# Two more loads of K at the head of the load queue of a decode kernel

## The chip, the core and the metric

The kernel runs on one core of a Trainium2 chip. The metric is the device time in microseconds (us) of one execution.

## The reference, cut to what matters

One decode step for two sequences: layernorm, attention of one new token over the last 2048 positions of a K and V cache (32 heads of 192), an output projection with a residual, then a second layernorm and a gated feed-forward part with its residual.

```
B, Sq, D = 2, 1, 640;  Hq = Hkv = 32;  Sk, Dh = 8192, 192;  F = 1536;  W = 2048
def attention(x, k_cache, v_cache, wq, wo):
    q = (x @ wq).reshape(B, Sq, 32, 192).transpose(0, 2, 1, 3)
    k, v = k_cache[:, :, Sk - W:], v_cache[:, :, Sk - W:]
    p = softmax(einsum("bhqd,bhkd->bhqk", q, k) * 192 ** -0.5)
    return einsum("bhqk,bhkd->bhqd", p, v).transpose(0, 2, 1, 3).reshape(B, Sq, 6144) @ wo
h = x + attention(layernorm(x), ...)
out = h + (gelu(n @ w_gate) * (n @ w_up)) @ w_down        # n = layernorm(h)
```

All inputs and the output are bf16. K and V of the window are 2 x 32 x 2048 x 192 values each, 50.3 MB apiece.

## The kernel before, in words

**Groups.** The 64 pairs of sequence and head are worked off in 16 groups g of four heads. The window's 2048 positions of one head are cut into 32 runs of 64 positions (`TPG`), and one run, 64 x 192 values, is 24,576 contiguous bytes in memory. A group's K is thus 32 x 4 runs, and each of the 128 partitions of SBUF gets one run: `kv_src` (L369 to L371) builds the source as `"h (i t) d -> i h (t d)"`, the run number i outermost, the head h next, so partition 4i + h holds run i of head h. V is loaded in the same way.

**The ring.** All big loads go into one tile, `ring`: 147,456 bytes per partition, six slots of 24,576 (`SLOT`). `K_AT` (L234) puts the K of groups 0 to 3, modulo four, at slots 0, 1, 3 and 5; `V_AT` puts V at slots 2 and 4. Wq (61,440 bytes per partition, `load_wq`) lies from the middle of slot 3 to the end of slot 5. Wo and the feed-forward weights later take slots that K and V have left.

**What sets the order.** The program is recorded first (`P.op`) and then emitted engine by engine; waits are worked out from what each operation reads and writes. `load` (L347) puts a load into a list. `pump` takes loads from its head, in order, as long as the ring space that they need is not held by a load that is still to be used; `done` marks a load as used and calls `pump` again. Every load in the ring is issued by SP (recorded at L363), on one queue, in the list's order. SP waits before an issue until what it overwrites is free: for the readers of the old contents, and, where a load lands on space that another load has written and nobody reads, for that other load's completion. The wait stands on SP, so all later issues stand behind it.

**The order of loads.** K(0), Wq, K(1), V(0), then K(g+1) and V(g) in turn, a quarter of Wo after every fourth group, and the feed-forward weights at the end. K(2) lands on space of Wq, so SP issues it only when PE has used Wq.

**Beside SP.** ACT's queue issues two small loads: the first fifth of W_gate (L394) and x (L431). POOL and DVE build constants (identities, masks) in the first 17 us. PE transposes each K group as pairs of bf16 (L574), DVE (L588) and ACT (L584) copy it out of PSUM; q is projected once from Wq (L598, in `q_rows`); scores, softmax and the product with V follow group by group; `oproj` adds a quarter of the output projection, then comes the feed-forward part. One store of the output (L878) ends the kernel: `out[:, 0, :].rearrange("b (r n) -> r b n", r=4)`, four blocks of two rows, from 8 partitions.

The list of loads begins (L430 to L434):

```
        load_wg0()
        P.op("act", lambda e: e.dma_start(xrow[0:2, :], A_x[:, 0, :]), W=["xrow"], dma="dx")
        load_k(0)
        load_wq()
        load_k(1)
```

## Time and profile before

| | |
|---|---|
| median of 2 runs | 292.64 us (292.55 to 292.73) |
| the profiled execution's own time | 292.58 us |
| its span, first to last instruction | 291.3 us |
| busy share of PE, PE weight loads, DVE, ACT, POOL | 68%, 51%, 42%, 26%, 9% |
| DMA packets | 6506, 122.44 MB, 420 GB/s over the span |
| read from memory | 122.29 MB |
| K loads, V loads | 16 and 16 of 3072 KB each |

Times below are in us from the start of the span. The page cuts the span into 40 slices of 7.3 us; each digit is a busy share in tenths, and a row GB/s gives what the 16 DMA engines moved. The DMA queue of SP is q1, that of ACT q10. SPq is SP's issuing of a DMA; the time behind it is that of the issue, not of the transfer. A DMA is split into packets: here one packet for each contiguous run of a load, and a small one for each DMA engine that reports its part as complete. In the timeline, what stands in brackets is how long the engine was idle before the row, and what ended that.

### The profile page before, as it was taken

The numbers are of one execution on the slowest core, as the hardware profiler recorded it, in microseconds if no ns is written. First come the engines' busy times: TensorE is split into PE (matmuls) and PEld (weight loads), VectorE is DVE, ScalarE is ACT, GpSimd is POOL, SyncE is SP. The second block draws the span as 40 slices with busy tenths as digits, with TensorE's granted clock in tenths as the row PEclk, the third lists the DMA queues.
The fourth block names the chain that finished last, engine by engine and source line by source line (L and its number), as shares of the span: only waits on it lengthen the run. The fifth ranks groups of instructions, "written<-read, shape, count | busy, mean of one in ns | idle before, by whom it ended". The sixth has DMA issues, their size and how long they took to land.

```text
span 291.3 us, 5093 instructions
## 1 busy us (share of the span) xinstructions
PE 198.6 (68%) x2141; PEld 147.6 (51%) x2141; DVE 122.8 (42%) x231; ACT 76.9 (26%) x72; POOL 25.7 (9%) x85
## 2 busy tenths in 40 slices
PE   0650868786668288768677478868478778496684
PEld 0640437566355175637374475645465746472341
DVE  4350025455435334635356244635247445253331
ACT  1050014333322122423222123523142333151001
POOL 8820073000000000000000000000000000000000
PEclk9997568999979869997989579999689799688957
DMA  8999999999999999999999999999999999999994
GB/s 324 432 440 422 428 432 432 428 429 429 428 419 440 432 432 432 429 432 432 432 416 448 432 432 430 432 412 429 432 432 425 422 432 432 429 432 434 420 411 181
DMA packets 6506, 122.44 MB, mean 420 GB/s; under 512 B 734, under 2 KB 864, under 8 KB 1504
## 3 DMA queue, kind: packets, MB, share of 16 engines
q1 hardware_dynamic: 6348, 121.90, 97.8%
q10 hardware_dynamic: 148, 0.40, 0.4%
q8 instruction: 7, 0.11, 0.2%
q14 instruction: 3, 0.02, 0.0%
HBM read 122.29 MB, written 0.00 MB: 420 GB/s over the span
## 4 chain that ended last, share of the span: by engine, by line
DMA 73%; PE 18%; DVE 3%; issue 2%; SPq 2%; ACT 1%; DVEq 0%
DMA ring<-in_A_k_cache_dram 54%; PE tpp L574 13%; DMA ring<-in_A_wq_dram 10%; DMA ring<-in_B_w_down_dram 9%; DVE ktr L588 3%; PE tpp L598 2%; SPq L363 2%; PE ops L680 1%; DVE ering L428 1%; ACT ktr L584 1%; PE m L731 1%; PE m L713 1%; PE m L871 0%; PE m L694 0%; DVE yrow L877 0%
## 5 line engine op out<-in xcount | busy, mean ns | idle before, releaser
L574 PE MATMUL tpp<-identf,ring 128*128 128x128 f32 x768 | 116.2, 314 | 39.3 <-DMA ring<-in_A_k_cache_dram 25.2
L574 PEld LDWEIGHTS tpp<-identf,ring 128*128 128x128 f32 x768 | 102.8, 163 | 47.5 <-DMA ring<-in_A_k_cache_dram 26.5
L588 DVE COPY ktr<-tpp 128x2048 bf16<-128x2048 bf16 x64 | 78.4, 1224 | 91.4 <-PE tpp L574 91.4
L584 ACT ACTIVATE ktr<-tpp 128x2048 bf16<-128x2048 bf16 x32 | 60.1, 1877 | 94.9 <-PE tpp L574 94.9
L655 ACT ACTIVATE eexp<-sm,nm 128x512 bf16<-128x512 f32 x16 | 11.6, 722 | 71.7 <-DVE nm L653 71.7
L635 PE MATMUL sps<-ktr,rq 128*16 128x512 bf16 x384 | 25.7, 402 | 1.1 <-POOL rq L428 1.1
L680 PE MATMUL ops<-ring,ering 128*32 128x384 bf16 x512 | 25.0, 339 | 0.0
L644 DVE CUSTOM_DVE_ANT_1 sm<-sps,mska 128x512 f32<-128x512 f32 x16 | 11.0, 686 | 27.0 <-issue 27.0
L428 POOL TENSOR_TENSOR rq<-qs,mask 128x96 bf16<-128x96 bf16 x16 | 5.5, 354 | 175.6 <-PE sps L635 154.1
L680 PEld LDWEIGHTS ops<-ring,ering 128*32 128x32 bf16 x512 | 12.7, 99 | 8.5 <-issue 2.8
L635 PEld LDWEIGHTS sps<-ktr,rq 128*16 128x16 bf16 x384 | 8.9, 89 | 14.4 <-issue 5.5
L651 PEld LDWEIGHTS m<-mrhs,pm 128*128 128x128 bf16 x16 | 1.5, 96 | 22.9 <-DVE mrhs L424 22.9
L651 PE MATMUL m<-mrhs,pm 128*128 128x16 bf16 x16 | 2.9, 184 | 14.8 <-DVE mrhs L424 14.8
L598 PE MATMUL tpp<-ring,xnT 128*32 128x384 bf16 x80 | 6.1, 499 | 9.4 <-DMA ring<-in_A_wq_dram 9.4
L598 PEld LDWEIGHTS tpp<-ring,xnT 128*32 128x32 bf16 x80 | 3.4, 143 | 11.9 <-issue 9.6
L621 DVE CAST qs<-ops 128x384 bf16<-128x384 f32 x1 | 0.6, 558 | 15.8 <-PE ops L616 15.8
L428 DVE TENSOR_TENSOR ering<-m,mask 128x256 bf16<-128x256 f32 x16 | 6.6, 415 | 1.3 <-PE m L664 1.3
L713 PE MATMUL m<-selb,orow 128*128 128x2 bf16 x48 | 3.5, 200 | 5.2 <-DVE ering L428 4.5
L713 PEld LDWEIGHTS m<-selb,orow 128*128 128x128 bf16 x48 | 3.2, 159 | 6.0 <-DVE ering L428 4.9
L664 PE MATMUL m<-sel,eexp 128*128 128x64 bf16 x64 | 4.8, 200 | 1.2 <-ACT eexp L655 1.2
L494 PE MATMUL m<-identb,xrow 2*128 2x2 bf16 x5 | 0.3, 173 | 7.4 <-DMA xrow<-in_A_x_dram 7.4
L428 DVE TENSOR_TENSOR orow<-m,wm 128x1536 bf16<-128x1536 f32 x3 | 5.3, 1751 | 0.0
(127 smaller groups left out, 93.6 us busy)
## 6 DMA issues: line engine op xcount, KB each, us to landing
ring<-in_A_k_cache_dram SPq DMA_DIRECT2D x16, 3072.0 KB, 29.5
ring<-in_A_v_cache_dram SPq DMA_DIRECT2D x16, 3072.0 KB, 25.4
ring<-in_A_wq_dram SPq DMA_DIRECT2D x1, 7680.0 KB, 28.1
ring<-in_A_wo_dram SPq DMA_DIRECT2D x4, 1920.0 KB, 21.6
ring<-in_B_w_gate_dram SPq DMA_DIRECT2D x1, 1536.0 KB, 31.4
ring<-in_B_w_up_dram SPq DMA_DIRECT2D x1, 1536.0 KB, 21.9
ring<-in_B_w_down_dram SPq DMA_DIRECT2D x1, 960.0 KB, 24.3
ring<-in_B_w_down_dram SPq DMA_DIRECT2D x1, 480.0 KB, 25.0
```

The lines of the kernel that those rows point to most:

```text
L363: P.op("sp", lambda e, v=v, src=src: e.dma_start(v, src), W=toks + [("sem", sem)], dma=sem)
L428: return lambda e: e.tensor_tensor(out=out, in0=a, in1=b, op=op)
L574: ins = e.transpose(tpp[bi][:, 512 * j + 128 * u:512 * j + 128 * (u + 1)], kv[:, off:off + 128], identf[:, :])
L584: act(lambda e, dst=dst, bv=bv: e.activation(out=dst, in_=bv, func=ACT.Copy), W=[("kt", half, k)], X=both)
L588: dve(lambda e, dst=dst, bv=bv: e.tensor_copy(dst, bv.rearrange("p (a x) -> p a x", a=2)), W=[("kt", half, k)], X=both, cls=0)
L598: ins = e.matmul(tps[0][32 * r:32 * (r + 1), 0:384], lhsT=xnT[:, c, 32 * J:32 * (J + 1)], rhs=wq[:, c, 1536 * J + 384 * r:1536 * J + 384 * ...
L635: ins = e.matmul(sps[32 * ch:32 * ch + 16, :], lhsT=rq[:, g % 4, k, :], rhs=ktr[:, k // 2, 1024 * ch + k % 2:1024 * (ch + 1):2], start=(k ...
L644: dve(lambda e: e.tensor_tensor_reduce(out=sm[:, :].rearrange("p (u x) -> p u x", u=4), in0=sps[:, :].rearrange("p (u x) -> p u x", u=4), ...
L655: act(lambda e: e.activation(out=eexp[:, :], in_=sm[:, :], func=ACT.Exp, bias=nm[:, 0:1], scale=1.0, accum_out=zr[:, g % 4:g % 4 + 1]), R= ...
L664: ins = e.matmul(o, lhsT=eexp[:, 128 * u:128 * (u + 1)], rhs=sel64[:, :], start=True, stop=True)
L680: ins = e.matmul(ops_[32 * r:32 * (r + 1), 0:384], lhsT=ering[:, g % 4, t, :], rhs=vv[:, 384 * t:384 * (t + 1)], start=(g % 4 == 0 and t < 4),
L713: ins = e.matmul(m2[:, 2 * kk:2 * kk + 2], lhsT=orow[:, :, kk:DH:12], rhs=selb[:, :], start=True, stop=True)
```

## The change

Two loads are put at the head of the list, ahead of `load_wg0()`:

```
+        runs = A_k_cache[0, 0:8, SKT - WIN:, :].rearrange("h (i t) d -> h i (t d)", t=2 * TPG)
+        load("p0", 0, 2 * SLOT, runs.rearrange("h i x -> i h x"), lambda v: v, "p0")
+        load("p1", 2 * SLOT, 2 * SLOT, runs, lambda v: v, "p1")
+        done("p0", "p1")
         load_wg0()
         P.op("act", lambda e: e.dma_start(xrow[0:2, :], A_x[:, 0, :]), W=["xrow"], dma="dx")
         load_k(0)
```

Both read the same data: the window of the first eight heads of sequence 0, in runs of 128 positions, 49,152 contiguous bytes, 16 runs per head, 128 runs together, one for each partition. p0 goes to slots 0 and 1 of the ring, and its source has the run number outermost (16 runs, then 8 heads). p1 goes to slots 2 and 3, and its source has the head outermost (8 heads, then 16 runs); two runs of one head that follow each other in it follow each other in memory, and heads lie 3,145,728 bytes apart. Nothing reads either load. `done` marks both as used at once, so the list goes on; as their space is written again, SP waits for p0 before it issues K(0) (slot 0), and for p1 before Wq (its first half slot is the second half of slot 3). K(1) (slot 1) and V(0) (slot 2) come after these. The order of the instructions on PE, DVE, ACT and POOL is that of before; SP has the two loads more, ahead of K(0). All line numbers of the later code grow by 4.

## The prediction

> **What bounds the kernel now.** I read the page's slices first, then the chain, then the head of the timeline, then the packets of single DMAs.

> ```profile
> span 291.3 us, 5093 instructions
> ...
> PE   0650868786668288768677478868478778496684
> ...
> DMA  8999999999999999999999999999999999999994
> GB/s 324 432 440 422 428 432 432 428 429 429 428 419 440 432 432 432 429 432 432 432 416 448 432 432 430 432 412 429 432 432 425 422 432 432 429 432 434 420 411 181
> ```

> The 16 DMA engines are at 9 tenths in all slices but the first and the last, and in most of these move 432 GB/s, which is 27.0 GB/s for each of the 16. PE has slices with a 0, a 2 or a 4. So no engine's work sets the time: the bytes do, 122.44 MB at this pace.

> ```profile
> DMA 73%; PE 18%; DVE 3%; issue 2%; SPq 2%; ACT 1%; DVEq 0%
> DMA ring<-in_A_k_cache_dram 54%; PE tpp L574 13%; DMA ring<-in_A_wq_dram 10%; DMA ring<-in_B_w_down_dram 9%; DVE ktr L588 3%; PE tpp L598 2%; SPq L363 2%; PE ops L680 1%; DVE ering L428 1%; ACT ktr L584 1%; PE m L731 1%; PE m L713 1%; PE m L871 0%; PE m L694 0%; DVE yrow L877 0%
> ```

> The chain says the same: three quarters are loads. Its 18% of PE are the steps at which PE frees a ring slot and SP issues the next load; while these run, loads issued earlier keep the DMA engines busy (the slices stay at 9), so they cost the end nothing.

> The head of the timeline shows where the two loads go in:

> ```profile
> 0.72 0.66 SPq L363 DMA_DIRECT2D ring<-in_A_k_cache_dram  x1
> ...
> 1.44 0.57 SPq L363 DMA_DIRECT2D ring<-in_A_wq_dram  x1
> ...
> 11.22 4.56 PE L574 MATMUL tpp<-identf,ring 128*128 128x128 f32 x24 [0.99 <-DMA ring<-in_A_k_cache_dram]
> ...
> 29.71 6.14 PE L598 MATMUL tpp<-ring,xnT 128*32 128x384 bf16 x80 [9.35 <-DMA ring<-in_A_wq_dram]
> ...
> 35.97 0.53 SPq L363 DMA_DIRECT2D ring<-in_A_k_cache_dram  x1
> ```

> PE starts its transposes 0.04 us after the first K has landed and projects q when Wq has landed (29.7); only then does SP issue the next K (35.97). Everything that is computed hangs on the landing of these loads.

> Last, what one DMA is split into. The first answer is the last 1.3 us, with only the store of the output in it; the second is 3.6 to 7.3 us.

> ```profile
> DMA packets 12, 0.00 MB, mean 2 GB/s; under 512 B 12, under 2 KB 12, under 8 KB 12
> ...
> q1 hardware_dynamic: 12, 0.00, 0.9%
> ```
> ```profile
> q1 hardware_dynamic: 64, 1.57, 99.4%
> q10 hardware_dynamic: 4, 0.00, 0.2%
> ```

> The store moves 8 rows of 320 B and leaves 12 packets: 8 of data and 4 small ones. In the second answer q10 carries the 2 rows of x in 4 packets. The ACT queue's whole total on the page is 148: 128 rows of W_gate, 2 of x, and 18 more, which is 16 + 2. So each DMA engine that takes part adds one completion packet: 16 engines for 128 rows, 2 for 2 rows, and 4, not 8, for the store, whose address pattern in memory begins with a dimension of 4.

> **The change part by part.** Durations are from the profiled execution, whose own time is 292.58 us with a span of 291.3; it stands 0.06 under the median of 292.64, so I add to 292.6.

> 1. Two DMAs (SP, L363), each 128 x 49,152 B = 6.29 MB. HBM read goes from 122.29 to 134.87 MB. The issue itself is 0.66 us in SP's queue for the first; the second issues while the first moves: 0.

> 2. p0, runs outermost: memory side 16 x 8 runs, ring side 128 rows. Sixteen engines, 8 packets of 48 KB each. The loads here have 24 KB (K and V) and 60 KB (Wq) runs, and both pass at 420 to 440 GB/s, slice by slice, so 48 KB lies between: 6.29 MB / 432 GB/s = 14.6 us. It is nothing less, as no row has more than 432 for long. The slowest row for 16 engines is W_gate's start, in 3 KB runs:

> ```profile
> 1.70:3.00 1.30, 0.00 (x0) 0.00 (x0) 1.24 (x5) 1.07 (x1) 1.30 (x1) 1.00 0.82 236
> 7.28:14.56 7.28, 4.85 (x25) 4.62 (x26) 2.42 (x8) 0.47 (x2) 6.16 (x23) 1.00 1.00 432
> ```

> (Last columns: DMA share, GB/s.) At 236 GB/s p0 would take 26.7. I take 14.6: its runs are between those of the second row's loads, 16 times those of the first row.

> 3. p1, heads outermost: memory side 8 x 16 runs, ring side 128 rows. By the store's 4 engines for a first dimension of 4, 8 engines: 27.0 x 8 = 216 GB/s, 29.1 us. Ends: 14.6 (all 16 engines) and, at half of W_gate's 236, 53.3. I take 29.1, by the store's row, since the engines' pace in the rows does not depend on what a packet holds above 24 KB.
> [...]

> 4. New waits. SP's issue of K(0) now waits for p0, as it writes the same slots; Wq waits for p1. Queued behind on SP: Wq, K(1), V(0). When p0 lands, p1 is still moving; when p1 lands, its 8 engines still have their half of K(0) before them: half of 3.15 MB at 216 GB/s, 7.3 us. An issue is 0.53 to 0.66 us, and the first packets of a load came some 2.4 us after the issue at 0.72. So both waits are covered: 0. Without that cover (were K(0) done), about 3 us.
> The other 8 engines run K(0)'s half early and then idle until Wq; they get ahead by about 5 us, which no load gains by, since each is complete only with its slower half.

> 5. What is hidden: only set-up work could hide anything, and it hangs on nothing that delays a load. The 25.7 us of POOL and layernorm now end before K(0) lands; PE's first transposes just move. At the end nothing changes: the last W_down parts land and PE needs them. 0.

> Sum: 14.6 + 29.1 = 43.7; 292.6 + 43.7 = **336.3 us**.

> **Rivals.**

> *Two engines share one way into the ring, both loads.* Every load of the trace has 128 or 32 as its first dimension; 16 and 8 have not been seen, so nothing shows that 16 consecutive engines with 8 neighbouring rows each (p0), or 8 with 16 (p1), do not meet. If they meet in pairs, each at half pace: p0 29.1, p1 58.3, and K(0)'s half on the idle engines meets p1 as well, 0 to 7.3 more. 292.6 + 87.4 to 94.7 = 380 to 387, in the middle 383.7. For it: the layouts are new. Against it: 432 GB/s in every load so far.
> [...]

> *Only p1 is halved.* 14.6 + 58.3 (+ 0 to 7.3): 365 to 373. It has the fewer engines and its runs lie 3.1 MB apart for the 8 at work at once. *Only p0:* 29.1 + 29.1: 350.9.

> *p1 is spread over all 16.* 14.6 + 14.6: 321.7. Against it: the store's 4 completion packets.

> *Not slower.* The loads would have to run in time in which DMA engines idle now. That is the 2.4 us before the first packet, the last 3 and the gaps, about 8 of 291.3 us; it decides only from 38 us on, which the row of nines excludes. The mechanism that is left is that the loads do not happen or that the second read of the same lines delays none of the others; 292.6.

> **How the numbers follow.** Forecast 336.3: 0.40. Both halved: 0.33 (no row against it but the older layouts). Only p1: 0.12. Only p0: 0.05. All 16: 0.06. Not slower: 0.02, half of it taken as faster, which has no mechanism beyond it. Slower than 388 (memory side): 0.02. The range takes the first four, 0.90: from 333 (336.3 less the 3 us that start and end leave open) to 388 (387.3 rounded up); leaving out the second case would leave less than 8 in 10. The forecast's own range is 333 to 340 (3 us more if a wait is not covered). Faster or slower by over 2% (5.9 us, about what a measurement of this kernel tells from no change): slower 0.98, within 0.01, faster 0.01.

> **What would show it.** q1's packets: 6348 + 128 + 16 + 128 + 8 = 6628 with 8 engines for p1, 6636 with 16. In SP's timeline K(0) is issued when p0 lands, at about 18 us, and Wq when p1 lands, at about 47; with pairs sharing, about 33 and 91 to 98. The first PE L574 starts at 11.2 + 43.7 = 54.9, L598 at 73.4. GB/s: 432 in the first slices, 216 for three slices (more while K(0)'s half runs along), then 432 to the end. The forecast is wrong if the two issues lie more than 30 us apart, or if 432 does not show before 18 us.

## The result, and the profile after

The changed kernel takes 388.5 us (388.43 to 388.56, two runs) against 292.64 before: 1.3275 times as long, 95% interval 1.3218 to 1.3332. 95.9 us were added; the forecast was 43.7, and the range, up to 388.0, missed by 0.5. What happened is the pace of the first rival: both loads went at about half of what was forecast (199 GB/s for 432, 103 for 216).

The page of the changed kernel, slices of 9.7 us:

```profile
span 387.2 us, 5095 instructions
...
DMA  9989974545799999999999999999999999999994
GB/s 208 239 179 188 142 122 102 122 91 112 270 451 411 418 437 426 429 433 419 433 426 439 429 426 433 423 438 432 425 432 429 437 429 426 434 429 426 425 413 163
...
q1 hardware_dynamic: 6628, 134.49, 91.7%
...
HBM read 134.88 MB, written 0.00 MB: 348 GB/s over the span
```

From the twelfth slice on, the rows are those of before: 9 tenths and some 430 GB/s. Everything that was lost lies in the first eleven slices. There the row DMA and the row GB/s part company: in the first three slices the DMA engines are at 9 and 8 tenths, as they were before, and yet move about 200 GB/s. So the DMA engines were busy here without moving 430 GB/s: a packet counts as busy for as long as it takes, and one of 48 KB mostly took 3.84 us in these slices, where 24 KB took 0.91 before. The packets (6628) are the number forecast for 8 engines in the second load, and the bytes are those of the two loads.

The timeline of the changed kernel, rows of SP and PE:

```profile
35.06 0.59 SPq L363 DMA_DIRECT2D ring<-in_A_k_cache_dram  x1
```
```profile
100.77 0.36 SPq L363 DMA_DIRECT2D ring<-in_A_wq_dram  x1
...
107.85 4.66 PE L578 MATMUL tpp<-identf,ring 128*128 128x128 f32 x24 [93.35 <-DMA ring<-in_A_k_cache_dram]
...
126.08 4.69 PE L602 MATMUL tpp<-ring,xnT 128*32 128x384 bf16 x80 [9.09 <-DMA ring<-in_A_wq_dram]
```

K(0) is issued when the first load has landed, at 35.06 (forecast 18, both-halved rival 33), Wq when the second has, at 100.77 (47; 91 to 98). The two issues lie 65.7 us apart, where more than 30 was to show the forecast wrong. PE starts its transposes at 107.85, 96.6 us later than before, and its projection of q 96.4 later. The rest follows unchanged.

Three stretches of the changed kernel (last columns: granted clock, DMA share, GB/s): the first load; the second with half of K(0) beside it; the second alone.

```profile
4.00:34.00 30.00, 1.50 (x9) 1.27 (x9) 1.54 (x8) 0.47 (x2) 10.62 (x34) 1.00 0.96 199
37.00:57.00 20.00, 0.00 (x0) 0.00 (x0) 0.00 (x0) 0.00 (x0) 0.00 (x0) 1.00 0.93 138
59.00:97.00 38.00, 0.00 (x0) 0.00 (x0) 0.00 (x0) 0.00 (x0) 0.00 (x0) 1.00 0.49 103
```

The share of 0.49 in the third row is 8 of 16 engines, all the time; 103 GB/s over 8 engines is 12.9 each, where 27.0 was forecast. In the first row it is 16 engines with 12.4 to 13. In single packets of the trace: 48 KB take mostly 3.84 us in the first load; in the second 5.5 us while K(0) runs (whose 24 KB then take 2.75 instead of 0.91), and 3.8 after that.

### The profile page after: what moved, and what is told of

Same layout as the page of the kernel before. It is cut to its first block, busy times and chain, and to the rows that moved or that the text cites. A ratio compares the mean times of both kernels' runs of the same rounds, so it can differ in the third digit from the quotient of the medians.

```text
span 387.2 us, 5095 instructions
## 1 busy us (share of the span) xinstructions
PE 197.0 (51%) x2141; PEld 147.2 (38%) x2141; DVE 122.8 (32%) x231; ACT 76.9 (20%) x72; POOL 25.7 (7%) x85
## 3 DMA queue, kind: packets, MB, share of 16 engines
q1 hardware_dynamic: 6628, 134.49, 91.7%
## 4 chain that ended last, share of the span: by engine, by line
DMA 63%; another core or an unknown queue 17%; PE 14%; DVE 2%; issue 2%; SPq 1%; ACT 0%; DVEq 0%
DMA ring<-in_A_k_cache_dram 50%; PE tpp L578 11%; DMA ring<-in_A_wq_dram 7%; DMA ring<-in_B_w_down_dram 6%; SPq L363 1%; DVE ktr L592 1%; PE tpp L602 1%; PE ops L684 1%; ACT ktr L588 0%; DVE ering L428 0%; PE m L735 0%; PE m L717 0%; PE m L698 0%; PE m L875 0%
## 5 line engine op out<-in xcount | busy, mean ns | idle before, releaser
L588 ACT ACTIVATE ktr<-tpp 128x2048 bf16<-128x2048 bf16 x32 | 60.1, 1877 | 190.6 <-PE tpp L578 190.6
L639 PE MATMUL sps<-ktr,rq 128*16 128x512 bf16 x384 | 24.6, 389 | 1.1 <-POOL rq L428 1.1
L428 POOL TENSOR_TENSOR rq<-qs,mask 128x96 bf16<-128x96 bf16 x16 | 5.6, 355 | 271.7 <-PE sps L639 155.2
L602 PE MATMUL tpp<-ring,xnT 128*32 128x384 bf16 x80 | 4.7, 407 | 9.1 <-DMA ring<-in_A_wq_dram 9.1
L428 DVE TENSOR_TENSOR ering<-m,mask 128x256 bf16<-128x256 f32 x16 | 6.7, 416 | 1.3 <-PE m L668 1.3
L735 PE MATMUL m<-ring,ot 128*2 128x320 bf16 x96 | 4.7, 340 | 1.2 <-DMA ring<-in_A_wo_dram 1.2
L428 DVE TENSOR_TENSOR orow<-m,wm 128x1536 bf16<-128x1536 f32 x3 | 5.3, 1751 | 0.0
```

What stands on the lines that cost most here:

```text
L428: return lambda e: e.tensor_tensor(out=out, in0=a, in1=b, op=op)
L588: act(lambda e, dst=dst, bv=bv: e.activation(out=dst, in_=bv, func=ACT.Copy), W=[("kt", half, k)], X=both)
L602: ins = e.matmul(tps[0][32 * r:32 * (r + 1), 0:384], lhsT=xnT[:, c, 32 * J:32 * (J + 1)], rhs=wq[:, c, 1536 * J + 384 * r:1536 * J + 384 * ...
L639: ins = e.matmul(sps[32 * ch:32 * ch + 16, :], lhsT=rq[:, g % 4, k, :], rhs=ktr[:, k // 2, 1024 * ch + k % 2:1024 * (ch + 1):2], start=(k ...
L735: ins = e.matmul(m1[32 * r:32 * r + 2, 192:512], lhsT=ot[:, kk, :], rhs=wo[:, kk - k0, 320 * h:320 * (h + 1)], start=(kk == 1 or J < 2 and ...
```

## The experiments

All of them compute the same as the kernel before; only the unused loads at the head differ. Two theories stood at the start: S, the ring side, and M, the memory side.

**Other addresses, same shapes.**

```
+flat = A_k_cache[0].rearrange("h s d -> (h s d)")       # blocks(a, b): a blocks of b runs, 4 KB between
+load("p0", 0, 2 * SLOT, blocks(16, 8), ...);  load("p1", 2 * SLOT, 2 * SLOT, blocks(8, 16), ...)
```

> Both loads keep their shapes (first dimension 16, then 8; 128 runs of 48 KB each) but read other data: the runs of one engine follow each other in memory, and engines start 397,312 bytes (first load) or 790,528 bytes (second) apart instead of 49,152 and 3,145,728. Theory S, the ring side (with a first dimension of 16 or 8 two engines at a time write through one way into SBUF): the addresses do not matter, packets of 3.84 us in the first load, 388 us as in the changed kernel. Theory M, the memory side (engines whose addresses lie a large power of two apart meet in memory): full pace, 1.81 us for a packet, 14.6 + 29.1 us added, 336 us.

389.15 us, 1.3295 times before (1.3256 to 1.3333). Its stretches are those of the changed kernel:

```profile
4.00:34.00 30.00, 1.50 (x9) 1.27 (x9) 1.70 (x8) 0.47 (x2) 10.63 (x34) 1.00 0.95 197
...
59.00:97.00 38.00, 0.00 (x0) 0.00 (x0) 0.00 (x0) 0.00 (x0) 0.00 (x0) 1.00 0.50 103
```

So it is not the distance in memory between the engines, and M in that form is out. The second load moves the same 103 GB/s with the 4 KB between its blocks and without.

**First dimension 32, same runs of 48 KB.**

```
+runs = A_k_cache[0, 0:8, SKT - 2 * WIN:, :].rearrange("h (i t) d -> i h (t d)", t=2 * TPG)    # 32 runs a head
+load("p0", 0, 2 * SLOT, runs[:, 0:4, :], ...);  load("p1", 2 * SLOT, 2 * SLOT, runs[:, 4:8, :], ...)
```

> The same bytes in the same runs of 48 KB, engines again 48 KB apart in memory, but the first dimension is 32 (32 runs of each of 4 heads, over the last 4096 positions; heads 0 to 3 in the first load, 4 to 7 in the second). S: full pace, 1.81 us a packet, 2 x 14.6 us added, 322 us. M: the pitch of the first load is kept, so both go at half pace like it, 3.84 us a packet, 2 x 30.7 added, 354 us. Also by a theory that runs of 48 KB are slow in themselves: 354 us.

321.69 us, 1.099 times (1.0958 to 1.1022): 29.0 us for the same 12.58 MB. In its trace a packet of 48 KB takes 1.815 us:

```profile
4.00:16.00 12.00, 1.50 (x9) 1.27 (x9) 1.54 (x8) 0.47 (x2) 10.22 (x33) 1.00 0.94 406
18.00:31.00 13.00, 0.00 (x0) 0.00 (x0) 0.00 (x0) 0.00 (x0) 0.00 (x0) 1.00 1.02 442
```

So neither the bytes nor the length of the runs cost more than forecast; of the 95.9 us, 29.0 are the bytes' own and 66.9 the price of the two shapes (K(0), which runs beside the second load, included).

**Heads outermost, but 32 rows at a time.**

```
+for m in range(4):
+    P.op("sp", lambda e, m=m: e.dma_start(two[32 * m:32 * m + 32, :], runs[:, 4 * m:4 * m + 4, :]), ...)   # 8 heads x 4 runs
```

> The first load as in the changed kernel; the second, heads outermost, is cut into four DMAs of 8 heads x 4 runs, each into 32 rows of the ring, so that engine h writes rows 4h to 4h+3 of a block of 32. Its runs and their addresses, 3.1 MB apart between the 8 engines, are the same. S: the eight engines write through eight different ways, full pace, 1.81 us a packet for 16 packets: 30.7 + 29.1 added, 352 us. M: nothing changes, 388 us.

352.13 us, 1.203 times (1.1995 to 1.2065). The first row is the first load, left as it was; the second the four DMAs after K(0)'s half:

```profile
4.00:30.00 26.00, 1.50 (x9) 1.27 (x9) 1.60 (x8) 0.47 (x2) 10.64 (x34) 1.00 1.02 210
46.00:62.00 16.00, 0.00 (x0) 0.00 (x0) 0.00 (x0) 0.00 (x0) 0.00 (x0) 1.00 0.50 215
```

Again half of the DMA engines (0.50), but 215 GB/s instead of 103: twice the pace for the same runs, from the same addresses, by the same number of engines. Only the rows that are written at any one time differ, and the cut into four DMAs, each of which still has a first dimension of 8.

**First dimension 16, runs of 24 KB.**

```
+runs = A_k_cache[0, 0:8, SKT - WIN:, :].rearrange("h (i t) d -> i h (t d)", t=TPG)
+load("p0", 0, SLOT, runs[0:16, :, :], ...);  load("p1", 2 * SLOT, SLOT, runs[16:32, :, :], ...)
```

> Both loads with a first dimension of 16 (16 runs x 8 heads), but in runs of 24 KB, the pitch of the kernel's own K loads; half the bytes. S: half pace, 1.92 us a packet of 24 KB, 2 x 15.4 added, 323 us. M (the pitch of 24 KB is that of the K loads, which run at full pace): 0.91 us a packet, 2 x 7.3 added, 307 us.

322.69 us, 1.1024 times (1.0992 to 1.1056).

```profile
5.00:16.00 11.00, 1.50 (x9) 1.27 (x9) 1.19 (x7) 0.47 (x2) 9.23 (x31) 1.00 0.99 208
```

These are packets of the size of the kernel's own K loads; they take 1.9 us, where K's own take 0.91. Half the bytes cost 30.0 us this way, where the whole 12.58 MB with 32 outermost cost 29.0.

In these four kernels the time by S, worked out from the packets of 3.84 us that the changed kernel had shown, is within 1.2 us of the measured one; the time by M is off by 15 us or more.

**One load alone.**

```
-load("p1", ...)        # the other kernel: -load("p0", ...); what is left goes to 2 * SLOT
```

> Only the load with the runs outermost, in slots 2 and 3, so that Wq waits for it and K(0) stands behind it. S: 8 packets of 3.84 us on each engine, 30.7 us added, 323.3 us. Rival W (what was added is mostly the waits and the order of the queue, not the packets' pace): the two loads alone don't add up to the 95.9 us of both; this one under 315.

323.13 us against 292.66 in the same series: 30.5 us.

> Only the load with the heads outermost, in slots 2 and 3; K(0) is issued right behind it and runs on the eight idle engines at the same time. S, with K(0) as a third on the same ways: four packets at 5.5 us and twelve at 3.83 on each of the 8 engines, 68 us added, 360.5 us. S without a meeting with K(0): 16 x 3.83 = 61.3 added, 354 us. W: under 350.

358.14 us (357.6 to 358.69): 65.5 us. Together 96.0, and the change added 95.9: the two prices add up, and W falls.

**The sharing by itself.**

```
+short = A_k_cache[0, 0:2, SKT - WIN:, :].rearrange("h (i t) d -> h i (t d)", t=TPG // 2)
+for n in (16, 32, 64):
+    load(("p", n), 0, SLOT // 2, short[:, 0:n, :], lambda v, n=n: v[0:2 * n, :], f"p{n}");  done(("p", n))
```

> The sharing by itself: ahead of all else three DMAs, one after the other, of 2 heads x 16, 32 and 64 runs of 12 KB, so that two engines write rows that lie 16, 32 and 64 apart at any one time; all go to slot 0, so each waits for the one before, and K(0) for the last. S with one way for rows 32 apart: 0.46 us a packet for the first, 0.96 for the second, 0.46 for the third, so 7.4 + 31 + 30 us and three waits of 2.5, all in all about 368 us. Rival F (few engines, or heads 3.1 MB apart, are slow in themselves): the same pace in all three; at 0.96 each 399 us, at 0.46 each 352.

360.68 us (359.99 to 361.38), and the three DMAs, with two engines each:

```profile
5.00:10.00 5.00, 1.17 (x4) 1.00 (x4) 1.09 (x6) 0.47 (x2) 3.88 (x15) 1.00 0.12 52
13.00:37.00 24.00, 0.00 (x0) 0.00 (x0) 0.00 (x0) 0.00 (x0) 3.19 (x7) 1.00 0.12 31
42.00:69.00 27.00, 0.00 (x0) 0.00 (x0) 0.00 (x0) 0.00 (x0) 0.00 (x0) 1.00 0.13 54
```

All three rows have the share of two busy engines (2 of 16 is 0.125). With rows 16 and 64 apart these move 52 and 54 GB/s, full pace; with rows 32 apart, 31. F is out: both heads and the number of engines are the same in all three, and the pace is not. The expected 368 was 7 us too much, nearly 6 of them because the packets of the second DMA do not all take 0.96 us; they lie between 0.46 and 0.97, 0.78 on average. Why they vary was not tested. In the change's loads they vary less: in the kernel with exchanged slots (below) three of four packets of the second load stay at 3.84 us and the fourth takes 3.5 to 3.6. Why every fourth is shorter was not tested either.

**Who is slowed of K(0).** Two kernels with half of the second load alone, heads 0 to 3, in rows 0 to 63 or 64 to 127; and the first of them with other data.

```
+load("p1", 2 * SLOT, 2 * SLOT, runs[0:4, :, :], lambda v: v[0:64, :], "p1")      # the other: v[64:128, :]
```

> The second load alone, cut to its heads 0 to 3: 4 heads x 16 runs into rows 0 to 63, four engines with 16 packets each; K(0) runs on the twelve idle engines at the same time. Its own pace by S: 3.83 us and more, 61 to 68 us added, 354 to 361. What is asked is who is slowed of K(0). S with a fixed engine for each way (K(0)'s rows 64 to 127 have engines and ways of their own): the packets of K(0) on eight of the idle engines take 0.91 us. Rival G (the sharing slows all that is in flight): all packets of K(0) beside it take 2 to 3 us.

357.06 us. (The trace does not name the engine of a packet; packets are put down to one engine where each starts as the last one ends.) Of K(0)'s packets on the twelve idle engines those of one engine take 2.85 us and those of the other eleven about 1.94; of the load's four engines two are at 5.5 us and two at 3.84.

> As the lower-half kernel, but into rows 64 to 127, the side of which K(0)'s own engines are all idle ones: now both pairs have a third (two of K(0)'s engines at 2.75 us, the load's four at 5.5 while K(0) runs). S alone: the other ten engines' packets of K(0) at 0.91 us. G with the pace of the slowest pairs: all of K(0) at 2.75 us, as in the changed kernel, where also both sides met K(0). G with a fixed price: 1.94 us as in the lower half. Time 355 to 361.

357.31 us. Most of K(0)'s packets now take about 2.84 us, on all twelve engines (many of each engine's first and last ones 2.2 to 2.6), and those of the load's four engines up to 5.6 while K(0) runs. The stretch of 9 to 20 us, first in the lower-half kernel, then in the upper-half one:

```profile
9.00:20.00 11.00, 1.50 (x9) 1.27 (x9) 1.23 (x7) 0.47 (x2) 6.45 (x21) 1.00 0.95 183
```
```profile
9.00:20.00 11.00, 1.50 (x9) 1.27 (x9) 1.20 (x7) 0.47 (x2) 6.44 (x21) 1.00 1.03 143
```

S alone had K(0) at full pace on eight or ten engines; that is wrong in both. G holds in kind, and not with a fixed price: the engines that by S have ways of their own went at about the byte rate of slowed ones. In the lower half, 24 KB in 1.94 us (12.7 GB/s) is the rate of the two engines with 48 KB in 3.84 (12.8), not of the two with 5.5 (8.9); in the upper half, 24 KB in 2.84 us (8.7) is near that of the load's engines with 5.6 (8.8).

```
+runs = A_v_cache[1, 16:20, SKT - WIN:, :]...        # else as the lower half
```

> As the lower-half kernel, but the load's data are V of the other sequence, heads 16 to 19, instead of the very heads of K that K(0) reads at the same time. Theory G-memory (K(0)'s packets on engines with ways of their own are slowed to 1.94 us since they read behind the slow engines at the same place in memory): K(0)'s packets there 0.91 us. Theory G-ring (they are held up on the way into SBUF, whatever is read): 1.94 us as before. The time 357 us in either case, set by the four engines of the load.

356.4 us, and K(0)'s packets are as before, 1.94 us on eleven engines and 2.85 on one: it does not matter whether the load reads where K(0) reads. G-memory, in the form that was expected, is out; that the hold-up is on the way into the ring is what is left of the two, and is not shown by itself.

**K(0) after the second load instead of beside it.**

```
-load("p0", 0, 2 * SLOT, ...);  load("p1", 2 * SLOT, 2 * SLOT, ...)
+load("p0", 2 * SLOT, 2 * SLOT, ...);  load("p1", 0, 2 * SLOT, ...)
```

> Both loads as in the change, but with their slots exchanged: the second load goes to slots 0 and 1, so K(0) is issued only when it has landed, and nothing runs beside it. If K(0) beside it is what stretches its first packets to 5.5 us (G or S alike), all its packets now take 3.83 us, 16 x 3.83 = 61.3 instead of 65.1 between the two landings, and K(0)'s packets 0.91; with DMA engines that idle for about 2.5 us until K(0) comes: 292.6 + 30.7 + 61.3 + 2.5 = 387 us. If the first packets take 5.5 us for a reason of their own: 394 us.

385.85 us, 1.3175 times (1.3119 to 1.3232). From the landing of the first load to that of the second it takes 59.7 us, against 65.7 in the change; no packet takes 5.5 us any more, and most of K(0)'s take 0.91. The stretch of the second load, then K(0):

```profile
37.00:92.00 55.00, 0.00 (x0) 0.00 (x0) 0.00 (x0) 0.00 (x0) 0.00 (x0) 1.00 0.48 101
98.00:102.00 4.00, 0.00 (x0) 0.00 (x0) 0.00 (x0) 0.00 (x0) 0.00 (x0) 1.00 1.02 436
```

Running K(0) beside the second load therefore cost 6.0 us there. Without it the DMA engines stood idle for 2.1 us, from the last packet to K(0)'s first at 95.91.

## Why the prediction was wrong

*What bounds the kernel: right.* The bytes' pace does; nothing else changed, and the loss went one to one into the time (96.4 at the projection of q, 95.9 in the time).

*Part 2, the first load at 14.6 us: wrong, and here the step failed.* It took its pace from the length of its runs ("48 KB lies between"). The runs of 48 KB do go at that pace, 29.0 us for two loads with 32 outermost; a first dimension of 16 cost 30.5 for one. By theory S that is because DMA engines that write at the same time share a way into the ring; S gave the times of the first four experiments to within 1.2 us, but no trace shows such a way. What the rows shown did not hold was a load whose first dimension is neither 32 nor 128. The text said so under the first rival and still took the rows as evidence for the new layout.

*Part 3, the second at 29.1: the number of engines right, the pace wrong.* Eight engines, by 6628 packets and a share of 0.49; but 12.9 GB/s each instead of 27.0. It is the same failed step, and it cost more here: 65.5 us instead of 29.1, where the first load cost 30.5 instead of 14.6. "The engines' pace in the rows does not depend on what a packet holds above 24 KB" is true of those rows and beside the point: in the three DMAs with two engines, all in packets of 12 KB, the pace was 31 GB/s with rows 32 apart and 52 and 54 with rows 16 and 64 apart.

*Part 4, the waits: right.* Both were covered. The idle time without cover was 2.1 us where I put about 3. But K(0)'s half, which I let run "early" at no price, met the second load and cost 6.0 us.

*Part 5, nothing hidden: right.* But the 25.7 us quoted there are POOL's busy time over the whole span; the set-up work is only a part of it.

*The rival "two engines share one way into the ring": right in its price.* No row before showed such a way, and it is the author's explanation still; that the pace about halves is measured, in both loads. Its sum, 87.4 to 94.7, is 1.2 short of 95.9, because "half pace" was taken exactly: 29.1 + 58.3 + 7.3. The measured pace is a little less: 48 KB in 3.84 us is 12.8 GB/s, 5% under half of 27.0. So the first load took 30.5 instead of 29.1, and the second, without K(0) beside it, 59.7 instead of 58.3; K(0) then cost 6.0 of the 7.3 allowed. That is also what the upper end of the range lacked. This rival had 0.33, less than the forecast's 0.40; the layouts new to the trace should have weighed more than the rows of old ones.

## What to carry to other kernels

In these runs a load's pace went with the order of its dimensions; by theory S that order sets which rows the DMA engines write at the same moment. For 128 rows, put 32 or 128 outermost (some 430 GB/s here), not 16 (197 to 210) and not 8 (101 to 103, with half of the engines). Read the row GB/s beside the row DMA: a high share with half of the usual rate (0.96 and 199 GB/s, where 1.00 and 432 stood before) says that packets take longer than elsewhere in the trace. So it was at W_gate's start too (0.82 and 236 GB/s), where single packets of 3 KB took up to 0.74 us and most 0.12. And where a change brings a shape that no row of the trace has, the rows of other shapes bound its price from one side only.

## What the runs showed that was not expected

A load at half pace also slowed a load beside it, on engines that by S share nothing with it. K(0)'s packets of 0.91 us took 1.94 on eleven engines while two of the load's four engines took 3.84 us a packet and the other two 5.5, and about 2.84 on all twelve when the load's four took up to 5.6 (the kernels with the lower and the upper half). The first of these held with other data too. Beside the four DMAs of 32 rows, where by S nothing shares, K(0)'s packets took 0.91. Why engines that by S have ways of their own fall to the pace of slowed ones, and in the first case to that of the faster two, is not settled: the trace names neither engines nor ways.
